# Seven block products for eight in the first MLP product of the last two groups, interleaved with the second products of the group before

## Chip, cores, metric

The kernel runs on one core of one Trainium2 chip. The metric is the device time of one execution in microseconds. A version's time is the median of its executions. Every version is timed in turns with the kernel before on the same chip. A ratio between two kernels is the mean time of the one's fast runs over the mean of the other's fast runs of the same rounds, so it is not quite the ratio of the medians quoted beside it.

## The reference

Causal linear attention with a decay per head, then a two-layer MLP with a tanh GELU over all 3072 tokens:

```python
# q, k, v: (4, 8, 768, 64); blocks of 64 tokens; lam: one decay per head
intra = (qb @ kb.T) * Dmask @ vb
inter = (qb * lam_pow) @ kv_state
out[block] = intra + inter
kv_state = lam_block * kv_state + (kb * rev_pow).T @ vb
# x = attention output as (3072, 512); w_in (512, 2048), w_out (2048, 512)
h = x @ w_in
g = 0.5 * h * (1 + tanh(c * (h + 0.044715 * h**3)))
return g @ w_out
```

## The kernel before

The attention runs in 24 steps, a step being 256 tokens of four heads. MLP work is cut into "pieces" that wait in a list, `filler`. The program puts them between the attention's instructions with `fill(n)`, so that TensorE always has matmuls. Tokens form seven groups. The last four have 512 tokens each. Each engine works through its own instructions in program order, as the traces show (in the change, a ScalarE copy whose matmuls were done at 139.0 us starts at 144.29 us, behind a gelu that was ahead of it in the program). PSUM is the memory in which the program's matmuls add up their results, bank by bank.

The first product of a large group is plain: for each of 16 blocks of 128 hidden features, four matmuls of 512 columns (128 input features each) are summed in one PSUM bank. ScalarE reads the bank, applies the GELU and writes `gT`:

```python
def mm1(fs):
    Hps = ps_M.tile([P, per, N], FP32, tag="M", name="Hps")
    for i, f in enumerate(fs):
        for c in range(NC):                       # 4 blocks of input features
            pin(nc.tensor.matmul(by_block(Hps[:, i, :]), w_in16[:, c, f * P : (f + 1) * P],
                                 x(c), start=(c == 0), stop=(c == NC - 1)))
    ...
    pin(nc.scalar.activation(out=dst, in_=Hps[:], func=AF.Gelu_apprx_tanh))
```

The second product is already done by seven block products for eight (Strassen's form): five sums of blocks of `gT`, five of `w_out`, and seven products of 256 columns. VectorE and ScalarE put the results together outside PSUM:

```python
PLACE = {4: ("A", 0), 3: ("A", 1), 5: ("B", 0), 2: ("B", 1), 1: ("C", 0), 7: ("D", 0), 6: ("D", 1)}
def product(m, p):
    ...                                            # 8 matmuls of 256 columns into one half of a bank
    if m == 2:                                     # ScalarE copies B, VectorE adds A: 512 elements
        ...
        pin(tt(banks["diag"], A[:], m525[:, 0:2], ALU.subtract))
        pin(tt(flat[:, 1:3], A[:], m525[:, 1:3], ALU.add))
    elif m == 1:
        pin(tt(d, banks["C"][:, 0].unsqueeze(1).to_broadcast([P, 2, HE]), d, ALU.add))
    ...
```

The last eight steps run in "bursts" of two:

```python
for n in range(16, NSTEP, 2):
    burst((n, n + 1), (15,) if n == 16 else (n - 2, n - 1))
    fill(2)
    U(n)                                           # state updates on VectorE and GpSimd
    U(n + 1)
    ...                                            # prep of later steps, more fill
burst((), (NSTEP - 2, NSTEP - 1))
fill(len(filler))
```

Of the kernel before, what the change touches and what calls it, by code (L numbers as in the profile page):

```python
# [15 lines left out]
def kernel(  # L16
# [12 lines left out]
    P = 128  # L29
# [30 lines left out]
    def load_step(s, names="qkv"):  # L60
# [3 lines left out]
        for nm, src in (("q", q), ("k", k), ("v", v)):  # L64
            if nm not in names:
# [13 lines left out]
    w_sum16 = w16p.tile([P, 5, HF, HE], FP16)  # L79
    W_SUMS = {3: ((0, 1), ALU.subtract, (1, 1)), 4: ((1, 0), ALU.subtract, (0, 0)),  # L80
              1: ((0, 0), ALU.add, (1, 1)), 7: ((1, 0), ALU.add, (1, 1)),
              6: ((0, 0), ALU.add, (0, 1))}
    w_slot = {m: i for i, m in enumerate(W_SUMS)}
    wstage = {}
# [35 lines left out]
    def sum_wout(j, m, eng):  # L120

        (f0, e0), op, (f1, e1) = W_SUMS[m]

        def rows(f, e):
            f = f * HF + 4 * j
            return w_out16[:, f : f + 4, e * HE : e * HE + HE]

        pin(eng.tensor_tensor(w_sum16[:, w_slot[m], 4 * j : 4 * j + 4, :], rows(f0, e0), rows(f1, e1), op))  # L128


# [86 lines left out]
    def prep(s):  # L217
        prep_qk(s)
        prep_v(s)
# [140 lines left out]
    def burst(ns, ss):  # L360
# [52 lines left out]
        if i == len(groups[g]) - 1:  # L413
            queue_group(g)
# [47 lines left out]

    groups = [[0, 1], [2], [3], [4, 5], [6, 7], [8, 9], [10, 11]]
# [3 lines left out]
    def queue_group(g):  # L467
# [25 lines left out]
        def mm2(tau, part):  # L493
# [8 lines left out]
            if O2[tau][1] < NF:  # L502
# [8 lines left out]
        G_SUMS = {5: ((0, 0), ALU.add, (0, 1)), 2: ((1, 0), ALU.add, (1, 1)),  # L511
                  1: ((0, 0), ALU.add, (1, 1)), 7: ((0, 1), ALU.subtract, (1, 1)),
                  6: ((1, 0), ALU.subtract, (0, 0))}
        G_PLAIN = {3: (0, 0), 4: (1, 1)}
        W_PLAIN = {5: (1, 1), 2: (0, 0)}
        gsum, pairs = {}, []

        def block(T, F, i):
            return gT[:, i, F, T * HN : (T + 1) * HN]

        def sum_g(i0, i1, ms=None):
            for m, ((T0, F0), op, (T1, F1)) in G_SUMS.items():
                if ms and m not in ms:
                    continue
                if m not in gsum:
                    k = len(gsum)
                    if k % 2 == 0:
                        pairs.append(wst.tile([P, 2, HF, HN], FP16, tag="w32", name=f"gs_{g}_{m}"))
                    gsum[m] = pairs[-1][:, k % 2]
                i = slice(i0, i1)  # L530
                pin(nc.vector.tensor_tensor(gsum[m][:, i, :], block(T0, F0, i), block(T1, F1, i), op))  # L531

        of_pair = {}
        PLACE = {4: ("A", 0), 3: ("A", 1), 5: ("B", 0), 2: ("B", 1), 1: ("C", 0), 7: ("D", 0),
                 6: ("D", 1)}

        def product(m, p):

            banks = of_pair.setdefault(p, {})
            name, half = PLACE[m]  # L540
            final = g == len(groups) - 1 and p == HN // P - 1
            if final and m == 6:
                name = "E"
            if m in (3, 5, 1, 7) or name == "E":
                banks[name] = ps_M.tile([P, 2, HE], FP32, tag="M", name=f"M{name}")
            dst = banks[name][:, half]
            t = slice(p * P, p * P + P)
            for i in range(HF):
                lhsT = block(*G_PLAIN[m], i)[:, t] if m in G_PLAIN else gsum[m][:, i, t]
                if m in W_PLAIN:  # L550
                    F, E = W_PLAIN[m]
                    rhs = w_out16[:, F * HF + i, E * HE : E * HE + HE]
                else:
                    rhs = w_sum16[:, w_slot[m], i, :]
                pin(nc.tensor.matmul(dst, lhsT, rhs, start=(i == 0), stop=(i == HF - 1),  # L555
                                     skip_group_check=True))
            tt = nc.vector.tensor_tensor
            if m == 2:
                o = banks["o"] = otp.tile([P, 2, 2, HE], FP32, tag="o32", name="o32")
                A, B = banks["A"], banks["B"]  # L560
                m525 = mtp.tile([P, 3, HE], FP32, tag="m525", name="m525")
                pin(nc.scalar.activation(out=m525[:, 0:2], in_=B[:], func=AF.Copy))  # L562
                pin(nc.scalar.activation(out=m525[:, 2], in_=B[:, 0], func=AF.Copy))
                flat = o[:].rearrange("p e t d -> p (e t) d")
                banks["diag"] = flat[:, 0:4:3]
                pin(tt(banks["diag"], A[:], m525[:, 0:2], ALU.subtract))  # L566
                pin(tt(flat[:, 1:3], A[:], m525[:, 1:3], ALU.add))
                if final:
                    for T, queue in ((1, nc.sync), (0, nc.scalar)):
                        row = row0 + T * HN + p * P  # L570
                        E = slice((1 - T) * HE, (1 - T) * HE + HE)
                        pin(queue.dma_start(out=out[row : row + P, E], in_=o[:, 1 - T, T, :]))
            elif m == 1:
                d = banks["diag"]
                pin(tt(d, banks["C"][:, 0].unsqueeze(1).to_broadcast([P, 2, HE]), d, ALU.add))
            elif final and m in (7, 6):

                o, T = banks["o"], (0 if m == 7 else 1)
                row = row0 + T * HN + p * P
                rows = out[row : row + P, :].rearrange("q (e d) -> q e d", e=2)  # L580
                d = o[:, T, T, :]
                pin(tt(d, banks[name][:, half], d, ALU.add))
                queue = nc.scalar if m == 7 else nc.sync
                pin(queue.dma_start(out=rows[:, T], in_=d))
            elif m == 6:
                d = banks["diag"]
                pin(tt(d, banks["D"][:], d, ALU.add))  # L587
                for T in range(2):
                    row = row0 + T * HN + p * P
                    pin(nc.sync.dma_start(out=out[row : row + P, :].rearrange("q (e d) -> q e d", e=2),  # L590
                                          in_=banks["o"][:, :, T, :]))
# [32 lines left out]
        for i in range(HF):  # L624
            for fs in ([[i, i + HF]] if per == 2 else [[i], [i + HF]]):
                filler.append(lambda fs=fs: mm1(fs))
        ms = ((3, 4, 5, 2), (1, 7, 6))
        order = [(m, p) for p in range(HN // P) for m in ms[0] + ms[1]]
        if g == len(groups) - 1:
            order = [(m, p) for part in ms for p in range(HN // P) for m in part]  # L630
        for m, p in order:
            filler.append(lambda m=m, p=p: product(m, p))

        def behind(k, i0, i1, ms=None):

            piece = filler[at + k]

            def both():
                piece()
                sum_g(i0, i1, ms)  # L640

            filler[at + k] = both

        at = len(filler) - len(range(HN // P)) * 7 - HF * (2 // per)
        n1 = HF * (2 // per)
        if per == 2:
            behind(5, 0, 4, (5, 2))
            behind(7, 4, 8, (5,))
            behind(8, 4, 8, (2,))
            behind(9, 0, 8, (1, 7))  # L650
            behind(10, 0, 8, (6,))
        else:
            behind(9, 0, 4)
            behind(13, 4, 6, (5, 2))
            behind(n1 - 1, 6, 8, (5,))
            behind(n1, 6, 8, (2,))
            behind(n1 + 1, 4, 8, (1, 7))
            behind(n1 + 2, 4, 8, (6,))

    def fill(n):  # L660
        for _ in range(min(n, len(filler))):
            filler.pop(0)()
# [17 lines left out]
    def U(n):  # L680
        update(n, 1)
# [65 lines left out]
    for m in (6, 3, 4, 1, 7):  # L747
        sum_wout(0, m, DVE)
    sum_wout(1, 6, DVE)
# [4 lines left out]
    sum_wout(1, 3, DVE)  # L754
# [10 lines left out]
    sum_wout(1, 4, DVE)  # L765
# [7 lines left out]
    sum_wout(1, 1, DVE)  # L773
    sum_wout(1, 7, DVE)
# [6 lines left out]
    for n in range(8, 16):  # L781
        stage_t(n)
        fill(1 if n == 9 else 0)
        prep_qk(n + 2) if n == 8 else prep(n + 2)
        fill({9: 1, 14: 3}.get(n, 2))
        R(n, n - 1)
        fill(1)
        U(n)
        if n == 8:
            prep_v(n + 2)  # L790
        fill(2 if n in (8, 11, 15) else 3)

    prep(18)
    fill(2)
    for n in range(16, NSTEP, 2):
        burst((n, n + 1), (15,) if n == 16 else (n - 2, n - 1))
        fill(2)
        U(n)
        U(n + 1)
        for m in (n + 3, n + 4):  # L800
            if m < NSTEP:
                prep(m)
            fill(4 if m % 2 == 0 and n % 4 == 0 else 6 if m % 2 == 0 else 6 if n % 4 == 0 else 10)
    burst((), (NSTEP - 2, NSTEP - 1))
# [29 lines left out]
```

## Time and profile before

| | before |
|---|---|
| time, median of 4 runs beside the change | 204.09 us (203.80 to 204.47) |
| profiled span | 202.2 us |
| TensorE busy | 194.2 us (96%) |
| VectorE busy | 145.7 us (72%) |
| ScalarE busy | 107.9 us (53%) |

The prediction below shows the lines of its profile and how they are read. One thing to know beforehand: TensorE's matmuls overlap, so that a matmul of 256 columns shows 273 ns of its own but follows the one before by 109 ns. The rate is read from the chain that ended last, or from start to start in the timeline. In the fences below, a timeline's columns are start (us), length (us), engine, line, operation, output<-inputs, shape, count, and in brackets the idle time before it with what ended it.

### The profile page before, as it was taken

To read this page: it belongs to the slowest core of one execution; us is meant where nothing else is said; L and a number is where in the kernel's file an instruction comes from. 1 tells how busy PE (TensorE), PEld (TensorE's weight loads), DVE (VectorE), ACT (ScalarE), POOL (GpSimd) and SP (SyncE) were. 2 spreads that over 40 slices of the span, in tenths; PEclk is the share of its full clock that TensorE was granted. 3 is DMA by queue.
4 is the path that set the end of the run, shared out by engine and by line. 5 is a ranking of instruction groups with operands and counts; after the bars stand their busy time and mean duration, and the time that the engine had idled before them with its cause. 6 is when DMAs were issued, how large, how long until landed. Compare 5 with 4: busy or idle time off the path is not lost.

```text
span 202.2 us, 5666 instructions
## 1 busy us (share of the span) xinstructions
PE 194.2 (96%) x2348; PEld 130.1 (64%) x2348; DVE 145.7 (72%) x293; ACT 107.9 (53%) x205; POOL 66.3 (33%) x80
## 2 busy tenths in 40 slices
PE   6888999999999999999999999999999999999993
PEld 1456544456888888645688764589664688544882
DVE  5896623889999999967799749899566462334753
ACT  2475778375893473477642368614367424466210
POOL 6594123457458264162531609303302000000000
PEclk9999999999999999999999999999999999999999
DMA  5999999999999999999875999306510003300014
GB/s 170 291 327 387 387 387 378 286 291 320 334 239 216 272 233 235 210 277 200 205 182 127 243 285 218 45 0 138 132 51 3 0 0 107 104 0 0 3 45 163
DMA packets 64201, 37.85 MB, mean 187 GB/s; under 512 B 17584, under 2 KB 59568, under 8 KB 64176
## 3 DMA queue, kind: packets, MB, share of 16 engines
q1 hardware_dynamic: 63344, 36.97, 72.1%
q10 hardware_dynamic: 832, 0.52, 0.8%
q8 instruction: 18, 0.29, 0.6%
q14 instruction: 7, 0.06, 0.1%
HBM read 27.26 MB, written 6.29 MB: 166 GB/s over the span
## 4 chain that ended last, share of the span: by engine, by line
PE 81%; DVE 6%; SPq 4%; DMA 4%; ACT 2%; issue 2%; DVEq 0%
PE Hps L484 37%; PE MB L555 8%; PE MA L555 8%; PE MD L555 7%; SPq L70 4%; PE MC L555 4%; DMA wi<-in_moe_w_in_dram 4%; PE Hps L601 3%; PE O2ps L499 3%; PE S L295 3%; DVE w_sum L128 2%; PE OK L353 2%; PE OK L344 1%; PE Tps L266 1%; DVE gs L531 1%
## 5 line engine op out<-in xcount | busy, mean ns | idle before, releaser
L484 PE MATMUL Hps<-xT,w_in 128*128 128x512 f16 (+1 forms) x416 | 78.7, 346 | 0.0
L488 ACT ACTIVATE gT<-Hps 128x512 f16<-128x512 f32 x88 | 52.3, 597 | 29.1 <-PE Hps L484 28.3
L484 PEld LDWEIGHTS <-w_in 128*128 128x128 f16 x416 | 40.4, 98 | 33.7
L531 DVE TENSOR_TENSOR gs<-gT 128x1024 f16<-128x1024 f16 (+1 forms) x62 | 40.8, 712 | 18.3 <-ACT gT L488 18.3
L456 POOL TENSOR_TENSOR u<-t,lumask 128x256 f16<-128x256 f32 x40 | 29.4, 749 | 67.0 <-DVE t L449 49.6
L555 PEld LDWEIGHTS <-gs 128*128 128x128 f16 x400 | 39.0, 98 | 4.5
L305 DVE TENSOR_TENSOR PT<-S,mask 128x512 f16<-128x512 f32 x48 | 30.4, 682 | 9.5 <-PE S L295 9.5
L230 POOL TENSOR_TENSOR v<-v,dv 128x512 f16<-128x512 f32 x24 | 28.5, 1194 | 5.0 <-DMA v<-in_v_dram 4.5
L555 PE MATMUL MA<-w_sum,gT 128*128 128x256 f16 x160 | 19.5, 273 | 0.4 <-DVE o L587 0.3
L555 PE MATMUL MB<-w_out,gs 128*128 128x256 f16 x160 | 19.1, 273 | 0.0
L248 ACT ACTIVATE qk<-k 128x512 f16<-128x512 f32 x24 | 15.0, 625 | 7.6 <-DMA k<-in_k_dram 7.6
L562 ACT ACTIVATE m<-MB 128x512 f32<-128x512 f32 x10 | 6.0, 597 | 23.4 <-PE MB L555 23.4
L555 PE MATMUL MD<-w_sum,gs 128*128 128x256 f16 x152 | 18.4, 273 | 0.0
L555 PEld LDWEIGHTS <-gT 128*128 128x128 f16 x160 | 15.4, 98 | 3.5 <-ACT gT L488 0.5
L243 DVE TENSOR_TENSOR qk<-q,dq 128x512 f16<-128x512 f32 x23 | 17.6, 767 | 0.0
L430 ACT ACTIVATE xT<-OK 128x256 f16<-128x256 f32 x29 | 11.1, 453 | 8.2 <-PE OK L353 7.9
L499 PE MATMUL O2ps<-w_out,gT 128*128 128x512 f16 x64 | 14.6, 379 | 0.0
L566 DVE TENSOR_TENSOR o<-MA,m 128x512 f32<-128x512 f32 x10 | 6.9, 689 | 9.6 <-ACT m L562 9.6
L128 DVE TENSOR_TENSOR w_sum<-w_out 128x1024 f16<-128x1024 f16 x10 | 9.1, 947 | 6.3 <-POOL w_out L118 3.5
L430 ACT ACTIVATE xT<-O 128x256 f16<-128x256 f32 x18 | 6.4, 458 | 10.4 <-PE O L404 7.5
L295 PEld LDWEIGHTS <-qkT 64*64 64x64 f16 x384 | 6.0, 106 | 7.0 <-issue 3.2
L449 DVE SCALAR_TENSOR_TENSOR t<-t,lamu,OK 128x64 f32<-128x64 f32 x44 | 10.1, 273 | 0.5
(68 smaller groups left out, 168.8 us busy)
## 6 DMA issues: line engine op xcount, KB each, us to landing
q<-in_q_dram SPq DMA_DIRECT2D x24, 256.0 KB, 5.3
k<-in_k_dram SPq DMA_DIRECT2D x24, 256.0 KB, 5.2
v<-in_v_dram SPq DMA_DIRECT2D x23, 256.0 KB, 5.2
out_dram<-o SPq DMA_DIRECT2D x22, 256.0 KB, 4.5
wo<-in_moe_w_out_dram SPq DMA_DIRECT2D x4, 1024.0 KB, 9.6
wi<-in_moe_w_in_dram SPq DMA_DIRECT2D x4, 512.0 KB, 7.6
wi<-in_moe_w_in_dram SPq DMA_DIRECT2D x2, 1024.0 KB, 12.7
v<-in_v_dram ACTq DMA_DIRECT2D x1, 256.0 KB, 4.4
```

Of the source, the lines that this page charges most:

```text
L128: pin(eng.tensor_tensor(w_sum16[:, w_slot[m], 4 * j : 4 * j + 4, :], rows(f0, e0), rows(f1, e1), op))
L230: pin(nc.gpsimd.tensor_tensor(wide(tv[:]), ld32[s][2][:], decay(dv, s), ALU.mult))
L243: pin(q_eng.tensor_tensor(wide(tq), q32[:], decay(dq, s), ALU.mult))
L248: pin(nc.scalar.activation(out=wide(tk), in_=k32[:], func=AF.Copy))
L305: pin(nc.vector.tensor_tensor(t[:, hl].rearrange("p b c d -> p b (c d)"), Sps[:].rearrange("p b c d -> p b (c d)"), mask[:].unsqueeze(1).t ...
L430: pin(nc.scalar.activation(out=d, in_=o, func=AF.Copy))
L456: pin(nc.gpsimd.tensor_tensor(u[:], state[half][:].unsqueeze(2).to_broadcast([P, 2, 2, D]), lumask[:, 2 * half : 2 * half + 2, :].unsqueez ...
L484: pin(nc.tensor.matmul(by_block(Hps[:, i, :]), w_in16[:, c, f * P : (f + 1) * P], x(c), start=(c == 0), stop=(c == NC - 1)))
L488: pin(nc.scalar.activation(out=dst, in_=Hps[:], func=AF.Gelu_apprx_tanh))
L499: pin(nc.tensor.matmul(O2[tau][0][:], gT[:, f % HF, f // HF, tau * P : (tau + 1) * P], w_out16[:, f, :], start=(n == 0), stop=(n == NF - 1)))
L531: pin(nc.vector.tensor_tensor(gsum[m][:, i, :], block(T0, F0, i), block(T1, F1, i), op))
L555: pin(nc.tensor.matmul(dst, lhsT, rhs, start=(i == 0), stop=(i == HF - 1), skip_group_check=True))
```

## The change

The intent: TensorE bounds the kernel, so take away matmuls. The first product of the last two groups also becomes seven block products for eight, in Winograd's form, with four sums of blocks on each side. A block of results comes out of running sums in PSUM: bank X takes products 1, 6, 7 and 4 one after the other and is read in between (u2 = products 1 + 6); bank W takes product 2; bank Y takes products 5 and 3. By the estimate in part 2 of the prediction these many reads would bound a stage by ScalarE (3.0 to 3.6 us of ScalarE a set, against 3.05 us of TensorE), so the pieces are interleaved ("merged") with the second products of the group before. The second product takes the same form in all groups but the first. Eight sums of blocks of `w_in` are made once, on VectorE. Some words for what follows: a "set" is one quarter of a group's hidden features, seven products of four matmuls each, so a group has four sets. A "half product" is four of the eight matmuls of one product of the second layer. A "g sum" is a sum of blocks of `gT`, an "input sum" one of blocks of the attention output. Core of the diff:

```diff
-    W_SUMS = {3: ((0, 1), ALU.subtract, (1, 1)), ...          # five sums
+    W_SUMS = {1: ((0, 1), ALU.subtract, (0, 0)), 2: ((1, 1), ALU.subtract, 1),
+              3: ((1, 1), ALU.subtract, (0, 1)), 4: ((1, 0), ALU.subtract, 2)}
+    def sum_win(m, j, eng): ...                               # the same for w_in
...
+        def seven(m, k):                                      # set k of 4, product m
+            dst = st[{2: "W", 5: "Y", 3: "Y"}.get(m, "X")]
+            for i in range(2):
+                for c in range(2):
+                    pin(nc.tensor.matmul(dst[:, i, :], ...))  # 256 columns
+            if m == 1:   copied("m1", "q32", nc.scalar)
+            elif m == 2: added(0, 0, "m1")                    # VectorE add, ScalarE gelu
+            elif m == 5: copied("q", "v32", nc.scalar)
+            elif m == 6: copied("u2", "k32", nc.vector)
+            elif m == 3: added(0, 1, "u2")
+            elif m == 7: added(1, 1, "q")
+            elif m == 4: gelu(1, 0, dst[:])
...
+        def merge(lead, per_set):                             # old: second-product halves
+            h(1)
+            for m in (1, 2, 3, 4): also(sum_x, m)
+            h(lead - 1)
+            for k in range(HF // 2):
+                for m in (1, 2, 5, 6, 3, 7):
+                    filler.append(lambda m=m, k=k: seven(m, k))
+                    if m == 1 and k > 0: filler.append(lambda k=k: seven(4, k - 1))
+                    h(slots[m])
...
+        paired = HN // P == 2                                 # W and Y share one bank
...
-    for n in range(8, 16): ...
+    for n, (a, b, c, d) in FILL.items():                      # single steps up to 17
+        if 11 <= n < 15:
+            for j in range(2): sum_win(n - 10, j, nc.vector)
...
+    burst((20, 21), (18, 19), 6, 5)
+    fill(4)
+    U(20)
+    U(21)
+    prep(23)
+    fill(52)
+    burst((22, 23), (20, 21))
+    U(22)
+    U(23)
+    fill(8)
+    burst((), (22, 23), 4, 4)
```

## The prediction

> **What bounds the kernel now.** I read the page first: busy shares, then the forty slices. The slices run from left to right over 202.2 us, each digit tenths of busy time; the last row is the granted clock.
>
> ```profile
> PE 194.2 (96%) x2348; PEld 130.1 (64%) x2348; DVE 145.7 (72%) x293; ACT 107.9 (53%) x205; POOL 66.3 (33%) x80
> ...
> PE   6888999999999999999999999999999999999993
> ...
> DVE  5896623889999999967799749899566462334753
> ACT  2475778375893473477642368614367424466210
> ...
> PEclk9999999999999999999999999999999999999999
> ```
>
> The reader is to see TensorE at 9 from the fifth slice to the last but one, and VectorE full only in patches. Since pipelined matmuls overlap, a busy digit does not prove full speed. I therefore took the chain that ended last, cut to the end of the kernel (start, length, what):
>
> ```profile
> 143.79 4.32 PE Hps L484 x20
> 148.11 0.57 PE S L295 x32
> ...
> 149.93 9.50 PE Hps L484 x44
> 159.42 1.75 PE MA L555 x16
> ...
> 172.77 13.81 PE Hps L484 x64
> 186.59 1.75 PE MA L555 x16
> ```
>
> Here 64 matmuls of 512 columns take 13.81 us, 0.2158 us each, and 16 of 256 columns 1.75 us, 0.109 us each. From 108 us to 198.8 us nothing but TensorE is in this chain: no gap to win, only work to remove. Before that there is little to win. In 39.7 to 118.5 us the groups by shape count 112 matmuls of 512 columns (24.2 us), 352 of 256 (38.4 us) and some 14.5 us of attention and transposes by their lengths in the chain: 77.1 of 78.8 us. At most 1.7 us is waiting, around 74 to 76 us (late gelu) and 99 to 108 us, where VectorE stands in the chain. The waits view, TensorE alone, confirms it: the largest wait after the start-up is this one.
>
> ```profile
> PE MA L555 <- DVE o L587: 0.3, 1, 0.3
> ```
>
> The tail after the last matmul is 202.2 - 198.8 = 3.4 us.
>
> [...] the trace's mean is 98 ns. So a 256-column matmul just covers its weight load, as it already does in the second product. [...] 1024 fp16 elements from SBUF and 512 fp32 elements from PSUM both took about 0.69 us when POOL was quiet. This matters, because the change adds PSUM adds. [...]
>
> **The change, part by part.**
>
> 1. TensorE, first product of the last two groups. Before, 16 output blocks by 4 contraction blocks = 64 matmuls of 512 columns = 13.81 us a group. After, 4 sets by 7 products by 2 by 2 = 112 matmuls of 256 columns, 112 x 0.109 = 12.2 us. Saved 1.6 us a group, **3.2 us** together, all on the path. The second product has seven products before and after (112 matmuls a group), so nothing is saved there.
>
> 2. Evacuation of the new first product, per set: ScalarE 2 copies and 4 gelus of 512 elements, VectorE one copy and 3 adds from PSUM. A lone ScalarE op takes 0.60 us, back to back about 0.50 (four gelus in 2.07 us), so 3.0 to 3.6 us a set. VectorE ops back to back come every 0.60 us (four mask products in 2.48 us), so 2.4 us a set. TensorE needs 28 x 0.109 = 3.05 us for a set: alone, ScalarE would bound. Interleaved with 5 or 4 half products (0.436 us each) of the preceding group, a set takes TensorE 5.2 or 4.8 us and both other engines fit on average.
>
> 3. Second product. Four sums instead of five: 2 x 0.60 us less VectorE time a large group. The results are summed in PSUM, so VectorE's 4 adds of 512 (0.69 each, 2.7 us) become 3 adds of 256 (0.42 each, 1.3 us) a pair; ScalarE gets 4 copies of 256 (0.38 each) for 0.60 + 0.38. About 1.4 us x 10 pairs less on VectorE. This lies beside TensorE, save near 99 to 108 us, where it may return up to 1 us.
>
> 4. Added on VectorE: eight sums of w_in (1024 fp16, 0.6 to 1.0 us each, 5 to 8 us) in four steps between about 70 and 95 us, and four input sums for each of the last two groups (512 fp16, 0.34 us each spaced, 1.4 us a group). The first lot lands where VectorE is 84 to 94% busy and takes back most of part 3 there.
>
> 5. Steps 16 and 17 become single steps. A single step took about 1.03 us of TensorE (0.35 + 0.12 + 0.23 + 0.33), a pair 1.82 us (0.57 + 0.45 + 0.25 + 0.55), so +0.2 us.
>
> 6. **The new wait.** I tallied VectorE's queue after the burst of steps 20 and 21, taking the burst of the kernel before as a model. Its timeline:
>
> ```profile
> 148.04 0.64 PE L295 MATMUL S<-qkT 64*64 64x128 f16 x32
> ...
> 148.50 2.48 DVE L305 TENSOR_TENSOR PT<-S,mask 128x512 f16<-128x512 f32 x4 [3.98 <-PE S L295]
> ...
> 149.76 9.66 PE L484 MATMUL Hps<-xT,w_in 128*128 128x512 f16 x44
> 149.85 1.38 ACT L430 ACTIVATE xT<-O 128x256 f16<-128x256 f32 x4 [1.11 <-PE O L404]
> 150.90 0.84 DVE L449 SCALAR_TENSOR_TENSOR t<-t,lamu,K 128x64 f32<-128x64 f32 x4
> ```
>
> From the burst's start VectorE is free at 3.7 us. After the change there follow, in program order, a g sum (4.3), four input sums (5.7), a g sum (6.3), four state updates at 0.19 (7.0), the q scaling (7.6), a g sum (8.2), a product add (8.6) and the first set's add of product 2 (9.2). ScalarE's first gelu waits for that add and, in order behind it, the copy of product 5, ready at about 10.4. TensorE starts its fillers at 1.7 and with 6 half products first, two sevens, a half, a seven, a half, a seven and a half reaches product 3 of the set at 7.4. Product 3 accumulates on the bank that the copy reads. So it waits **about 3 us**, once; VectorE's backlog is then gone. I give that 1.5 to 3 us, since the order may be kinder than my tally.
>
> 7. Chain inside a set. From product 7 to product 4 lie 0.87 us of TensorE, against about 0.9 us for matmul end, add and release. From product 5 to 3 lie 1.3 us (0.87 in the last group), against a ScalarE queue of gelu, copy, evacuation. I expect 0.1 to 0.3 us a set, 0.5 to 2 us over eight sets, plus up to 0.5 us at the end of the last merge, where no half product is left to cover product 7's add.
>
> Sum: -3.2 (part 1) - 0.5 (parts 3, 4) + 0.2 (part 5) + 1.5 to 3 (part 6) + 0.7 to 2.5 (part 7) = -1.3 to +2.0. The finely set leads and slots suggest that somebody balanced these waits on the chip, so I lean to the kinder end, and predict -1.3: **203.0 us**.
>
> **Rivals.** First, the work leaves TensorE and nothing comes back: -3.2 - 1 + 0.2, about 200.3 us. For it: averages of VectorE and ScalarE fit in each merged set, and the last 50 us had VectorE at 25.0 of 49.1 us and ScalarE at 22.2. Against it: the queue of part 6, and accumulators that are read halfway through. Second, **VectorE becomes the bound of the first merge**: its work there is 16 x 0.60 evacuations, 9 sums at 0.60, 6 product adds at 0.33, 1.4 of input sums, 0.8 of updates, 0.6 of q, 19.8 us, plus the 2.2 us left of the burst when the merge starts, against 56 x 0.436 = 24.4 us of TensorE: 90%. With ScalarE in order behind it, each adding waits, the merges could lose 5 to 7 us: 206 to 208 us. Third, the weights of w_in sums delay the middle of the kernel, where VectorE is already full: 0 to 2 us. More weight loads (112 for 64 a group) are no rival: at 98 ns they stay under 109 ns.
>
> **Range and chances.** The first rival without its 1 us, and with some luck, gives the low end, 200.6; the sum's pessimistic end 206.2. Faster by over 2% needs under 200.3 us, more than the arithmetic saves: 0.07. Slower by over 2% needs over 208.4: 0.07. Within: 0.86.
>
> **What would show each step.** Part 1: 224 matmuls of 256 columns in the two first products, in place of 128 of 512, and in stretches without waits 0.109 us each. Part 3: VectorE adds of 256 elements and about 0.42 us. Part 6: in the chain of waits, one TensorE gap of 1.5 to 3 us in the first set of the first merge, with a ScalarE copy and behind it a VectorE add as releasers. Part 7: small repeated gaps, product 3 behind a ScalarE copy and product 4 behind a VectorE add. Wrong if the middle of the kernel loses time to the w_in sums, if bank reuse holds TensorE at the merges' edges, or if the gaps of part 7 reach 0.5 us a set.

## The result

The change made the kernel slower: 215.43 us, median of 4 runs (214.64 to 216.66), against 204.09 us; ratio 1.0546 (95% interval 1.0500 to 1.0593). The profiled span is 214.9 us. The first rows of the page, in forty slices as in the prediction:

```profile
PE 197.9 (92%) x2444; PEld 141.7 (66%) x2444; DVE 157.7 (73%) x314; ACT 121.4 (56%) x241; POOL 67.8 (32%) x80
...
PE   6989999999999998999799999929998999998992
...
PEclk9999999999999999999999999985999999999999
```

There are 96 more matmuls, and TensorE's row is no longer a wall of nines. It falls to 2 in one slice, and in this slice and the next the granted clock falls to 8 and 5 tenths. What TensorE waited for, in the view of waits (total us, times, longest us):

```profile
PE MWY L598 <- DVE o L610: 5.0, 4, 3.3
PE HY L672 <- ACT q L683: 2.1, 5, 0.7
...
PE HX L672 <- DVE q L693: 1.2, 3, 0.7
PE MX L598 <- DVE gs L567: 0.7, 1, 0.7
```

Before, no such row exceeded 0.3 us after the start-up. L598 is the second product, L672 the new first product. The longest wait stands in the first set of the first merge. This is its timeline, with lines left out:

```profile
138.43 0.60 PE L672 MATMUL HY<-xs,ws 128*128 128x256 f16 x4
139.30 0.60 PE L672 MATMUL HX<-xs,ws 128*128 128x256 f16 x4
139.40 0.69 DVE L567 TENSOR_TENSOR gs<-gs,gT 128x1024 f16<-128x1024 f16 x1
140.00 0.85 DVE L472 SCALAR_TENSOR_TENSOR t<-t,lamu,K 128x64 f32<-128x64 f32 x4
140.77 1.00 DVE L266 TENSOR_TENSOR qk<-q,dq 128x512 f16<-128x512 f32 x1
141.69 1.09 DVE L567 TENSOR_TENSOR gs<-gT,gs 128x1024 f16<-128x1024 f16 x1
142.71 0.41 DVE L610 TENSOR_TENSOR o<-MWY,m 128x256 f32<-128x256 f32 x1
143.05 0.67 DVE L693 TENSOR_TENSOR m<-HW,m 128x512 f32<-128x512 f32 x1
143.18 1.01 PE L598 MATMUL MWY<-w_sum,gs 128*128 128x256 f16 x4 [3.28 <-DVE o L610]
143.76 0.63 ACT L689 ACTIVATE gT<-m 128x512 f16<-128x512 f32 x1 [5.41 <-DVE m L693]
144.29 0.58 ACT L683 ACTIVATE q<-HY 128x512 f32<-128x512 f32 x1
144.92 1.01 PE L672 MATMUL HY<-xT,ws 128*128 128x256 f16 x4 [0.73 <-ACT q L683]
145.73 1.06 PE L598 MATMUL MWY<-w_sum,gs 128*128 128x256 f16 x4
146.58 1.06 PE L672 MATMUL HX<-xs,ws 128*128 128x256 f16 x4
149.91 0.60 PE L672 MATMUL HW<-xT,w_in 128*128 128x256 f16 x4
```

VectorE never rests from 139.4 to 143.7 us; TensorE does. VectorE first does a g sum, the state updates, the q scaling and another g sum, and only then the add that frees the bank of W and Y (L610). ScalarE sits idle for 5.4 us behind the gelu that needs the add after it, and the copy of product 5 stands behind that gelu. When TensorE comes back, pieces of four matmuls start 0.85 us apart in place of 0.44. The windows view gives the granted clock there (after POOL: clock, DMA share, GB/s; before it the busy time of each engine):

```profile
132.00:139.70 7.70, 7.70 (x153) 6.39 (x152) 6.67 (x15) 4.48 (x10) 1.63 (x2) 1.00 0.28 36
139.70:143.20 3.50, 0.22 (x3) 0.05 (x2) 3.50 (x9) 0.00 (x0) 2.59 (x3) 0.97 0.02 4
143.20:150.00 6.80, 6.07 (x29) 4.08 (x29) 3.44 (x6) 3.24 (x6) 0.49 (x1) 0.51 0.20 37
150.00:168.00 18.00, 16.93 (x151) 14.27 (x150) 12.25 (x21) 11.33 (x22) 0.00 (x0) 1.00 0.09 30
```

For 6.8 us after the idle stretch of 3.28 us the clock is half: 0.51, against 1.00 in the 7.7 us before the stretch and in the 18 us after the slow part. That the slow clock belongs to the idle stretch is seen in e4_clock below, where matmuls fill most of the stretch and the clock stays at 1.00. The prediction had not counted on a change of the clock.

In all, the first merge took from 134.66 to 167.9 us, 33.2 us for 56 pieces of 0.437 us (24.5 us). The second took 176.40 to 198.36 us, 22.0 us for 44 pieces (19.2 us).

### The profile page after: what moved, and what is told of

Its sections match the earlier page's. It is cut to its first block, busy times and chain, and to the rows that moved or that the text cites. A ratio compares the mean times of both kernels' runs of the same rounds, so it can differ in the third digit from the quotient of the medians.

```text
span 214.9 us, 5981 instructions
## 1 busy us (share of the span) xinstructions
PE 197.9 (92%) x2444; PEld 141.7 (66%) x2444; DVE 157.7 (73%) x314; ACT 121.4 (56%) x241; POOL 67.8 (32%) x80
## 4 chain that ended last, share of the span: by engine, by line
PE 73%; DVE 14%; ACT 5%; issue 3%; DMA 2%; POOL 1%; DVEq 0%; ACTq 0%
PE Hps L520 22%; PE MX L598 13%; PE MWY L598 7%; PE O2ps L535 6%; PE HX L672 5%; PE Hps L757 3%; PE S L318 3%; DVE gs L567 3%; PE HY L672 3%; PE OK L376 2%; PE Tps L289 2%; PE OK L367 2%; DVE m L693 2%; DVE q L693 2%; DVE PT L328 2%
## 5 line engine op out<-in xcount | busy, mean ns | idle before, releaser
L520 PE MATMUL Hps<-xT,w_in 128*128 128x512 f16 (+1 forms) x288 | 50.8, 332 | 0.0
L524 ACT ACTIVATE gT<-Hps 128x512 f16<-128x512 f32 x56 | 33.1, 597 | 11.4 <-PE Hps L520 10.8
L598 PEld LDWEIGHTS <-gs 128*128 128x128 f16 x320 | 31.7, 99 | 10.7 <-issue 5.6
L598 PEld LDWEIGHTS <-gT 128*128 128x128 f16 x240 | 23.2, 98 | 3.3 <-ACT gT L524 0.5
L598 PE MATMUL MX<-w_sum,gs 128*128 128x256 f16 x160 | 21.6, 273 | 0.7 <-DVE gs L567 0.7
L567 DVE TENSOR_TENSOR gs<-gT 128x1024 f16<-128x1024 f16 (+1 forms) x24 | 16.6, 692 | 2.4 <-ACT gT L689 1.4
L672 PEld LDWEIGHTS <-ws 128*128 128x128 f16 x128 | 12.8, 100 | 5.5 <-issue 3.6
L598 PE MATMUL MWY<-w_sum,gs 128*128 128x256 f16 x64 | 9.6, 299 | 5.0 <-DVE o L610 5.0
L672 PEld LDWEIGHTS <-w_in 128*128 128x128 f16 x96 | 9.8, 102 | 3.7 <-issue 1.8
L693 DVE TENSOR_TENSOR m<-HW,m 128x512 f32<-128x512 f32 x8 | 5.5, 689 | 7.6 <-ACT m L683 5.4
L598 PE MATMUL MX<-w_sum,gT 128*128 128x256 f16 x80 | 10.5, 272 | 0.0
```

Of the source, the lines that this page charges most:

```text
L567: pin(nc.vector.tensor_tensor(g_rows(m, i), g_rows(a, i), g_rows(b, i), op))
L598: pin(nc.tensor.matmul(dst, lhsT, rhs, start=(opens and i == 0), stop=(closes and i == HF - 1), skip_group_check=True))
L672: pin(nc.tensor.matmul(dst[:, i, :], w_in_block(a, slice(c, c + 1), slice(f * P, f * P + P))[:, 0], x_block(b, slice(c, c + 1))[:, 0], sta ...
L693: pin(nc.vector.tensor_tensor(st[name], dst[:], st[name], ALU.add))
```

## Experiments

Thirteen kernels ran. All gave right results. Five undo or isolate parts, the others follow the waits. One warning on small differences: the first long run of first-product matmuls (32 of 512 columns) began between 24.8 and 26.5 us in the profiles of kernels whose start-up code is the same. So a single execution can differ by over a microsecond for no reason of the change, and single profiled spans are not compared below. Where two profiles are compared, it is by the "stretch" from the first matmul of that long run to the first matmul of the kernel's last product: 182.8 us in the change. Two kernels with the same code up to the burst of steps 22 and 23 (e2_eight_sums and e8_last) still differ by 0.4 us up to there, so differences of that size say nothing. Times of kernels from different rounds are each good to about 1 us by their intervals.

### e1_eight and e2_eight_sums: what is left when nothing is merged

```diff
-    SEVEN = (5, 6)
+    SEVEN = ()
-    fill(52)
+    fill(22)
     burst((22, 23), (20, 21))
...
-    fill(8)
+    fill(10)
# e1_eight only: the sum_win calls are taken out as well
```

> The changed kernel with the first product of the last two groups again by eight (64 matmuls of 512 columns a group), not interleaved, and without the sums of w_in; the new form of the second product and the new step order stay. Theory A (the loss of 11 us is made in the merged stages): 204 to 205.5 us, TensorE near full speed from 118 us to the end. Theory B (the new second product, its shared banks and the new order of steps cost much): 207 us or more.

> As e1_eight, but the eight sums of w_in stay (their results unused). The difference to e1_eight is what the sums cost in the middle. Theory A: 0 to 1 us, a TensorE wait of about 0.7 us near 82 us. Theory B' (the sums fill VectorE and delay the middle): 2 us or more over e1_eight.

Measured: e1_eight 206.28 us (ratio to before 1.0106, interval 1.0066 to 1.0145), e2_eight_sums 207.90 us (1.0191, 1.0155 to 1.0227). Neither hit its figure. Of the 11 us, the new form of the second product with its schedule costs 1.9 us and the sums of `w_in` another 1.6 us (1.8 us by the stretches, 173.2 and 175.0 us). About 0.7 of the 1.9 us is the tail: from the last matmul to the end pass 4.1 us, and 3.4 us in the kernel before. The waits of TensorE in e1_eight and then in e2_eight_sums:

```profile
PE MWY L598 <- DVE o L610: 1.2, 2, 0.8
```

```profile
PE MWY L598 <- DVE o L610: 2.4, 3, 1.0
...
PE MX L598 <- DVE gs L567: 0.7, 1, 0.7
```

The first is the shared bank again: W and Y are two halves of one tile, and TensorE's first write of Y waits until VectorE has read W (0.8 us at the longest in e1_eight). That sharing makes the program wait is shown by e10_eight_tuned below; it separates tile and bank at once, so which of the two the wait hangs on is not shown. The second pair shows what the sums of `w_in` do: one before a g sum that a product needs (0.7 us), the others before the add that frees the bank (1.2 us more).

### e8_last: only the last group merged

```diff
-    SEVEN = (5, 6)
+    SEVEN = (6,)
...                                      # fills: 22 before the burst of (22, 23), 12 after it
```

> The changed kernel with only the last group's first product by seven, merged with the second products of the group before it; the first of the two merges is undone, the sums of w_in stay where they were. Against e2_eight_sums (207.9 us, no merge) it tells what the second merge is worth: by the traces it saves 1.6 us of matmuls and has about 2.8 us of gaps, so 1.2 us over, about 209. If the first merge makes nearly all of the loss, and the second pays: 206.3.

Measured: 210.34 us (1.0303, 1.0263 to 1.0343), 2.4 us over e2_eight_sums in spite of 1.6 us of matmuls saved. So by the times the second merge alone has about 4 us of losses, more than I had expected. The stretch gives less: 176.8 us, 1.8 us over e2_eight_sums, so 3.4 us of losses, of which 0.4 us lies ahead of the merge, where the code is the same. The first merge then adds the other 5.1 us to the 215.43 us of the change, or 6.0 us by the stretches. The parts 1.9, 1.6, 2.4 and 5.1 us make 11.0 of the 11.3 us measured; the split between the two merges is good to about 1 us.

### e3_late: VectorE's queue ahead of the first set

```diff
-    U(20)
-    U(21)
-    prep(23)
-    fill(52)
+    fill(13)
+    U(20)
+    U(21)
+    prep(23)
+    fill(39)
```

> The changed kernel with the state updates of steps 20 and 21 and the q scaling of step 23 moved behind the first set of the first merge. Theory C (VectorE's queue in front of the first set's add makes the 3.3 us gap, and the gap makes the clock drop to half): the gap shrinks by the 1.85 us that these took, to 1.2 to 2 us, the clock stays whole, in sum 3 to 5 us less, 210 to 212.5 us. Theory D (the set's chain through ScalarE makes the gap whatever VectorE has queued): within 1 us of the changed kernel's 215.4.

Measured: 213.84 us (1.0458, 1.0409 to 1.0508), 1.6 us less than the change. The gap did shrink to the size expected, but three things ate the gain. Timeline of TensorE:

```profile
138.31 0.60 PE L672 MATMUL HX<-xs,ws 128*128 128x256 f16 x4
140.22 0.60 PE L598 MATMUL MWY<-w_sum,gs 128*128 128x256 f16 x4 [1.30 <-DVE o L610]
141.96 1.01 PE L672 MATMUL HY<-xT,ws 128*128 128x256 f16 x4 [1.15 <-ACT q L683]
142.77 1.06 PE L598 MATMUL MWY<-w_sum,gs 128*128 128x256 f16 x4
...
146.29 0.60 PE L672 MATMUL HX<-xT,w_in 128*128 128x256 f16 x4 [0.96 <-DVE t L472]
```

The wait for ScalarE's copy grew to 1.15 us. A new wait of 0.96 us came up: the second set's bank was still held for the state updates, which I had moved behind it. And two gaps of 1.5 and 1.3 us from matmul to matmul, with one piece between, were followed by a halved clock as well: from 142 to 145 us it was 0.50. The queue theory holds for the gap itself. My sum for its removal was too good.

### e4_clock: the clock alone

```diff
+        def dummies():
+            hbank["X1"] = ps_M.tile([P, 2, SB], FP32, tag="M", name="HX")
+            for _ in range(12):
+                pin(nc.tensor.matmul(hbank["X1"]..., ones[:, 0:P], ones[:], start=True, stop=True))
...                                      # run once, behind product 6 of the first set
```

> The changed kernel with 12 matmuls of ones of 512 columns (2.6 us) laid into the gap, into a bank that the next set overwrites; all else as it was. If the halved clock after the gap costs 2 us by itself: the seven pieces that took 0.85 us each take 0.44 and the total falls by 1.5 to 2.5 us, to about 213.3. If the clock drop is only a symptom that other waits would have covered: no change, or 0.3 us more.

Measured: 214.00 us (1.0490, 1.0436 to 1.0543), 1.4 us less than the change. The timeline shows the dummies, and after them the next pieces at 0.44 us:

```profile
139.83 2.75 PE L715 MATMUL HX<-ones 128*128 128x512 f16 x12 [1.00 <-DVE t L472]
142.42 0.60 PE L598 MATMUL MWY<-w_sum,gs 128*128 128x256 f16 x4
143.85 0.60 PE L672 MATMUL HY<-xT,ws 128*128 128x256 f16 x4 [0.83 <-ACT q L683]
144.29 0.60 PE L598 MATMUL MWY<-w_sum,gs 128*128 128x256 f16 x4
144.72 0.60 PE L672 MATMUL HX<-xs,ws 128*128 128x256 f16 x4
```

The clock was whole (1.00) in every window asked, from 138 to 164 us. In the change six pieces (not seven, as the expectation says) took 5.0 us, from 144.92 to 149.91 us; here the same six take 2.7 us, from 143.85 to 146.54 us. So the clock cost 2.3 us by the trace, and the stretch is shorter by as much (180.5 us). By the times it is 1.4 us, with runs that overlap a little (213.29 to 215.08 against 214.64 to 216.66). Adding useless work to an idle TensorE made the kernel no slower, and rather faster.

### e5_order: the order inside the sets

```diff
-                for m in (1, 2, 5, 6, 3, 7):
+                for m in (1, 2, 5, 6, 3, 7) if first_set else (1, 5, 2, 6, 3, 7):
                     filler.append(lambda m=m, k=k: seven(m, k))
-                    if m == 1 and k > 0:
+                    if m == 5 and k > 0:
                         filler.append(lambda k=k: seven(4, k - 1))
...                                      # one half product moved to the end of a merge
```

> The changed kernel with one other order inside the sets (all but each merge's first): products 1, 5, 4 of the set before, 2, 6, 3, 7 in place of 1, 4, 2, 5, 6, 3, 7, and two half products instead of one ahead of each merge's last product 4. The ScalarE copy of product 5 then no longer stands behind a gelu that waits for VectorE, and product 4 comes 0.44 us later behind product 7. If the chain inside the sets costs what the repeated gaps sum to (0.1 to 0.9 us each, 2.5 us from the second set of the first merge on, and 1.2 in the last three sets of the second): 2 to 3 us less, about 212.8. If the gaps come from a shortage of VectorE or ScalarE: no change within 1 us.

Measured: 214.37 us (1.0483, 1.0423 to 1.0543), 1.1 us less than the change, with overlapping runs: by time alone inconclusive, and short of the 2 to 3 us expected. The stretch is 1.4 us shorter (181.4 us), although the wait ahead of product 3 in the first set grew from 0.73 to 1.15 us. The waits are clearer: in the second merge the change had five waits (0.38, 0.51, 0.25, 0.25 and 0.35 us), this kernel two (0.38 and 0.31 us). So these gaps came from the order in ScalarE's queue and not from too little time on either engine.

### e6_start: the start of the first merge

```diff
-    burst((20, 21), (18, 19), 6, 5)
+    burst((20, 21), (18, 19), 12, 4)
...                                      # input sums behind half 6, U(20), U(21) behind half 12
+    fill(10)
+    prep(23)
```

> The changed kernel with only the start of the first merge changed: 12 half products ahead of the first set in place of 6 (then 4 a set), the input sums behind the sixth of them, the updates of steps 20 and 21 behind the twelfth, the q scaling of step 23 behind the first set, two g sums later. By the queue theory VectorE then reaches the adds in time: no gap over 1 us in the first set, the clock stays whole, 5 to 6 us less, about 209.5 to 210.5. By the rival (VectorE as the bound of the whole merge) the wait comes back in later sets: less than 2.5 us gained.

Measured: 212.74 us (1.0400, 1.0362 to 1.0439), 2.7 us less than the change, short of the 5 to 6 us expected and just over the 2.5 us that the rival allowed. The gap of 3.3 us became two of 0.79 and 1.36 us. Both were second-product pieces waiting for the shared bank, now ahead of the sets. The clock stayed at 0.997 on average.

### e7_all: these together

Edit: e5_order and e6_start; `w_in` sums in steps 12, 13, 16 and 17; own banks for W and Y outside the merges (`paired` only for groups 4 and 5).

> Both of these, the sums of w_in in steps 12, 13, 16 and 17 instead of 11 to 14, and own banks for the two accumulators of a pair in the groups that aren't merged. If the causes are separate and add up: 5.5 + 2.5 + 1.6 us less than 215.4, about 206; if removed waits come back elsewhere: 208 to 211.

Measured: 210.14 us (1.0293, 1.0225 to 1.0362), inside the second range expected, 208 to 211 us. Waits for the shared bank (2.7 us, three times) remained in the merged groups, and a new 1.0 us came from `w_in` sums put in step 16, ahead of the adds that the last group-3 products needed. At the start of the first merge two waits of 0.8 and 1.4 us, with eight matmuls between them, left the clock at 1.00 (137 to 145 us).

### e10_eight_tuned, e9_last_tuned and e11_last_tuned2: banks, then the second merge

```diff
# e10_eight_tuned = e1_eight with
-        paired = HN // P == 2
+        paired = HN // P == 2 and g + 1 in SEVEN
-                    store(1, 1)
+                    store(1, 1, nc.scalar)
# e9_last_tuned = e10 with SEVEN = (6,), e5_order, and one w_in sum behind each of
# eight first-product pieces ahead of the burst of (22, 23)
# e11_last_tuned2 = e9 with
-                    if k >= 2 and sums and m in (2, 6, 7) and len(old) <= unread[sums[0]]:
+                    if k >= 2 and sums and m in (2, 7) and len(old) <= unread[sums[0]]:
...              # order 1, 5, 2, 6, 3, 7 in every set; one half product ahead of the last product 4
+        paired = False
```

> e1_eight (nothing by seven in the first product) with own banks for the two accumulators of a pair and the one store moved. If the shared bank made the 1.2 us of waits and the store order 0.5 us of the tail: 206.3 falls to about 204.6. If the waits only move to another releaser: 205.8 to 206.5.

> As e8_last, with the order inside the sets of e5_order, the sums of w_in in the quiet stretch before the burst of steps 22 and 23, own banks for the two accumulators of a pair in the groups that are not merged, and one late store on ScalarE's queue. If the causes found are all: -1.6 us of matmuls and under 1 us of gaps against e10_eight_tuned, so 0.5 to 1 us faster than that and 203.5 to 205 us in all. If the waits come back elsewhere: 206 or more.

> As e9_last_tuned, but the order 1, 5, 2, 6, 3, 7 also in the first set, no g sum between product 6 and product 3, one half product kept for the end of the merge, own banks in all groups. The gaps of e9_last_tuned's merge (0.4 to 0.5 us, 0.4 us and 0.5 us in the trace) should go: 0.8 to 1.3 us less, 203.1 to 203.5. If they return behind other releasers: 204 to 204.5.

Measured: e10_eight_tuned 204.04 us (1.0001, 0.9969 to 1.0032), 2.2 us under e1_eight and level with the kernel before; TensorE waits for no bank any more (of the 1.2 us in e1_eight no row is left). With its accumulators apart and one store moved, the new second product costs nothing measurable. No run parts the two edits, but the profiles do: the stretch is 1.8 us shorter than in e1_eight (171.4 against 173.2 us), and the tail, where the moved store lies, 0.6 us (3.5 against 4.1 us). e9_last_tuned 204.36 us (1.0012, 0.9980 to 1.0044): the second merge no longer loses, and does not yet gain. e11_last_tuned2 **202.99 us** (202.75 to 203.03) against 203.78 us before (203.46 to 205.65), ratio 0.9945 (0.9907 to 0.9983): faster than both kernels, by 0.55% of the one before (0.4% by the medians, since two of the eleven runs before took over 205 us). That is a small gain, under 2%. Its merge ran from 164.45 to 184.95 us. Inside it the rate is that of TensorE:

```profile
168.81 0.60 PE L672 MATMUL HX<-xT,w_in 128*128 128x256 f16 x4
169.25 0.60 PE L672 MATMUL HY<-xs,ws 128*128 128x256 f16 x4
...
173.62 0.60 PE L672 MATMUL HX<-xT,w_in 128*128 128x256 f16 x4
...
177.91 0.60 PE L672 MATMUL HX<-xs,ws 128*128 128x256 f16 x4 [0.20 <-DVE u L685]
```

From product 1 of one set to product 1 of the next lie 4.81 us, which is 44 matmuls at 0.109 us. The merge takes 20.5 us for 45 pieces, 0.85 us over, so that about 0.75 of the 1.6 us saved is left. The stretch agrees: 170.5 us, against 171.4 us in e10_eight_tuned, which merges nothing.

### e12_both_tuned2 and e13_both_tuned3: the first merge by the same rules

```diff
# e12: both groups merged, own banks, e11's order; the burst of (20, 21) four pieces earlier
-    fill(4)
-    burst((20, 21), (18, 19), 6, 5)
+    burst((20, 21), (18, 19), 15, 4)
# e13: the burst back behind the four pieces, 11 half products ahead of the first set
```

> Both merges with the same rules, and the burst of steps 20 and 21 brought four pieces (3.45 us) forward so that VectorE works off its mask products beside plain first-product matmuls. If the first merge's loss was all of these removable waits: 1.6 us of matmuls less than e11_last_tuned2 and under 1 us of gaps, 202 to 203.5. If the first merge stays short of VectorE or of accumulator banks: 205 or more.

> As e12_both_tuned2, with the burst of steps 20 and 21 back in its old place and 11 half products ahead of the first set. If only the order made the loss: the 1.4 and 1.9 us waits and some 1.7 us of halved clock go, 202 to 203.5, no slower than e11_last_tuned2. If VectorE is short in the first merge: its backlog after the burst returns as waits of 1.5 us or more for accumulators or input sums there, 204 to 206.

Measured: e12_both_tuned2 207.37 us (1.0169, 1.0129 to 1.0209). The sets ran well, 25.4 us for the merge (136.98 to 162.38 us), 0.9 us over its 56 pieces, but the burst now came too early. TensorE's waits:

```profile
PE Hps L520 <- DVE PT L328: 1.9, 1, 1.9
...
PE S L318 <- DMA qkT<-qk: 1.4, 1, 1.4
```

The clock fell to 0.66 on average in the 5 us after them. e13_both_tuned3, with the burst back in its place, took 204.69 us (203.95 to 205.57; ratio 1.0030, 0.9998 to 1.0061): 10.7 us under the change, level with the kernel before at best, 1.7 us over e11_last_tuned2. The longest waits of TensorE in the first merge end on VectorE:

```profile
138.03 0.60 PE L672 MATMUL HY<-xs,ws 128*128 128x256 f16 x4 [0.90 <-DVE o L610]
138.96 0.60 PE L672 MATMUL HW<-xT,w_in 128*128 128x256 f16 x4 [0.34 <-DVE o L610]
```

The windows view of e13 (span, then busy time of TensorE, weight loads, VectorE, ScalarE, GpSimd):

```profile
130.00:141.60 11.60, 10.36 (x178) 8.96 (x178) 11.33 (x26) 5.17 (x12) 3.20 (x5) 1.00 0.17 24
141.60:159.00 17.40, 16.70 (x150) 14.34 (x147) 13.42 (x23) 12.13 (x25) 0.62 (x1) 1.00 0.17 47
```

From the burst on, VectorE is busy for 11.33 of 11.60 us, and TensorE waits 0.90 and 0.34 us for banks that VectorE's adds free. After that VectorE has room. So the time falls in the range expected if VectorE is short (204 to 206 us), though each wait stays under the 1.5 us named there; that VectorE's backlog makes the whole loss is not shown. Whether an order exists in which the first merge pays stays open: I tried three starts for it and found none. What is shown is that with these orders it wins nothing, while the second does.

## Why the prediction was wrong

The prediction set 3.2 us of matmuls saved against 1.9 to 5.2 us lost in parts 3 to 7. The saving came as forecast; the losses were 14.5 us (11.3 + 3.2). The steps that failed are parts 3 and 4, 6 and 7:

**The bound (right).** TensorE bounded the kernel, and there was no gap to win after 118 us. e11_last_tuned2 gained by taking matmuls away, with the waits removed.

**Part 1 (right in size).** Matmuls went as counted. Where nothing waited, the new ones came 0.109 us apart.

**Parts 3 and 4 (sign wrong).** The step said "-0.5". Measured: +1.9 us for the second product with its schedule (e1_eight) and +1.6 us for the sums of `w_in` (e2_eight_sums). I counted the VectorE time saved and missed that W and Y of a pair share a bank, so that a late VectorE add holds TensorE: with banks of their own (e10_eight_tuned) the stretch shrinks by 1.8 us. The tail grew by 0.7 us, which no part had. I also weighed the sums of `w_in` as load, where it is their place in the queue that counts.

**Part 6 (queue right, path and size wrong).** VectorE's queue after the burst did hold TensorE (e3_late). But the tally led from there through the set's add, the gelu and the copy to 3 us at product 3, with a ScalarE copy as releaser. It came as 3.28 us one piece earlier, at the shared bank, with a VectorE add of the second product as releaser, and only 0.73 us at product 3 behind the copy. That add stood in the tally, at 8.6 us after the burst's start (it ended at 10.2 us, 143.12 - 132.96), but not as something that TensorE waits for. I then gave it 1.5 to 3 us and no clock. The halved clock behind it cost 1.4 us by the times of e4_clock and 2.3 us by the trace. In all the first merge cost 5.1 us net (from e8_last to the change; 6.0 us by the stretches), so 6.7 to 7.6 us of losses against 1.6 us saved.

**Part 7 (too small).** I allowed 0.7 to 2.5 us for the chains in both merges and the end. The second merge alone lost 3 to 4 us: 1.8 us more than e2_eight_sums by the stretches and 2.4 us by the times, with 1.6 us saved. Its trace in the change shows 2.7 us over its 44 pieces (22.0 us in place of 19.2).

**Leaning (wrong).** "somebody balanced these waits on the chip, so I lean to the kinder end" was no evidence from the profile. It moved the figure against my own tally. Without it the sum's top, +2.0, would still have missed +11.3 us, since parts 3, 4 and 7 and the clock were missing.

**Rivals.** The second one named the loss best ("each adding waits"), but put the loss at 206 to 208 us and the cause in VectorE's total load. The totals fitted; the order did not. e13_both_tuned3 does the same work in another order, with other banks, and is 10.7 us faster. The third rival was right with 1.6 us inside its 0 to 2 us.

## What to carry to other kernels

When work moves from the bounding engine to engines that "fit on average", write down each in-order queue at the point of change and ask which entry frees a bank or lets the bounding engine go on: it must stand ahead of everything that can wait (here the add that frees the bank stood behind two g sums, the state updates and the q scaling, and TensorE waited 3.28 us). Keep accumulators that different engines touch at different times in tiles and banks of their own (1.8 us in e10_eight_tuned), and count an idle stretch of TensorE not only as itself but with the slow clock behind it: here 3.28 us of it cost another 2.3 us by the trace. Shorter waits in a row went both ways: two gaps of 1.5 and 1.3 us with one piece of 0.44 us between were followed by clock 0.50 (e3_late), 1.4 and 1.9 us with a burst between by 0.66 on average over 5 us (e12_both_tuned2), and 0.8 and 1.4 us with eight matmuls between by 1.00 (e7_all); what decides it is not shown. Merge where the other engines have room: here the last group paid (VectorE busy for 15.63 of the 20.50 us of its merge in e11_last_tuned2) and the one beside the attention did not (11.33 of 11.60 us from the burst on in e13_both_tuned3), in the orders tried.
